# A gated linear attention and GELU FFN kernel: halved first load, full-width inter products, a fixed instruction list

## Chip, cores and metric

The kernel runs on one core of a Trainium2 chip. The metric is device time in microseconds, from launch to end. Its parts are TensorE (PE in the profile; PEld are its weight loads), VectorE (DVE), ScalarE (ACT), GpSimd (POOL), and SyncE (SP), which issues most of the DMA transfers. PSUM has eight banks of 128 x 512 float32 that TensorE writes into.

## The reference

Four batches, eight heads, 768 tokens, head size 48. A state of 48 x 48 per head decays per key channel and is read by the query; the result, 3072 tokens of 384, goes through an FFN of width 2048.

```python
f = 1.0 / (1.0 + np.exp(-f_logit))
for t in range(S):
    state = f[:, :, t, :, None] * state + np.einsum('bhd,bhe->bhde', k[:, :, t], v[:, :, t])
    y[:, :, t] = np.einsum('bhd,bhde->bhe', q[:, :, t], state)
x = y.transpose(0, 2, 1, 3).reshape(B * S, H * D)
h = x @ w_in
out = (0.5 * h * (1.0 + erf(h / sqrt(2)))) @ w_out
```

## The kernel before

The 3072 tokens are 24 chunks of 128; two chunks are a unit (0 to 11), and two chunks are also a group of the FFN (0 to 11). Six chunks, three units, make a batch, so chunks 0, 6, 12 and 18 start without a state. Matmuls take bf16.

In a chunk the recurrence becomes matmuls. Cumulated log decays g come from a triangular matmul. k times exp(-g) and q times exp(g) are formed, scores are k against q under a triangular mask, and y is masked scores times v plus q times the old state (the **inter** product). The state adds the chunk's k-v product and is scaled by the chunk's whole decay.

Every piece of work is recorded in a plan with engine, estimated duration, priority and the buffers it needs. `Plan.run` picks, in before, the piece that can start first by its estimates, priority deciding between near ones (with random offsets from `SEEDS`). The result is emitted as one fixed order for each engine. Each engine runs its own in order, so a piece that waits holds back all behind it on that engine. The names of the pieces, with chunk or unit number, are used below:

- E, L (lines 494, 497, ACT): exp and log of the logits of a unit, giving log decays. C (526, 527, 515 or 521, 523, PE): their cumulated sums. G (535, DVE): the second chunk's sums by subtraction, units 2 to 4.
- RG, GT, GL (543, 549, 570 or 565, ACT): exponentials for k, q and the state. KP, QP (576, DVE or POOL): the decayed k and q, in buffers sc. VC (583, POOL or ACT): v cast to bf16, buffers vb.
- Tk, Tq (611, PE): transposes into PSUM. KQ (617, DVE or ACT): the copy to buffer kq. From unit 4 on both are a DMA transpose instead, KD (599, issued by SP).
- A (784 or 722, PE): scores. AM (631, DVE): mask. S (806 or 745, PE): the k-v product of the state. R (651, 655, DVE), T (657, POOL), SB (662, POOL, two head halves): state sum, decay and bf16 copy.
- YI (826), YX (705): the masked product and the inter product of units 0 to 4; Y (758 and 699) both, for the others. YB (675, DVE or ACT): y to bf16. XT, X (691, 694) or a DMA transpose XD (679): y transposed for the FFN.
- F1.g.u (875): an eighth of the first FFN layer of group g, six matmuls of 256 columns into one of four PSUM banks. GE (885, ACT): GELU of that bank. F2.n.r (896): a quarter of the second layer of chunk n, four matmuls of 384 columns. O (901): the copy out of PSUM. Stores (906) go out on SP.

Units 0 to 4 (`PAIRS`) are pair units: each SBUF row holds two consecutive tokens, even and odd, so that loads move runs of 384 bytes; the two 64-row halves of a tile are then the two chunks. Units 5 to 11 are loaded chunk by chunk. In a pair unit kq holds, for each of the even and odd tokens, 128 columns of which 64 belong to each chunk. The inter product of a chunk therefore takes two matmuls of 64 columns for each of four head pairs:

```python
for j in range(2):
    nc.tensor.matmul(yp.t()[64 * j:64 * j + 64, 96 * p:96 * p + 96],
                     kq.t()[:, 1, p, j, 64 * cc:64 * cc + 64], osb.t()[:, p, :], ...)
```

Loads are issued in the order of `LOADS`: for unit 0 the logits (f0), then k0, v0, q0, then f1, v1, k1, q1, then on GpSimd the first weight piece i0 (1024 of the 2048 columns), and so on. `load` gates a change of issuing engine on an earlier transfer, so that i0 waits for f1, i1 for k2, and the logits f3 for weight piece o3.

ScalarE needs one function table for exp and log and another for GELU, so its order is made of stages of one kind with a table load (line 953) between. Filler matmuls on a zero tile (line 947, called junk) are put before pieces that the plan expects to start late in the first 30 us.

Of the kernel before, what the change touches and what calls it, by code (L numbers as in the profile page):

```python
# [15 lines left out]

# [8 lines left out]

SPREAD, SEED = (1.0, 97)

SEEDS = [1643, 41, 3215, 1275, 2533, 2502, 823, 887, 1264, 763, 2447, 3095]

NUDGE = {}  # L30
XA = 0.0
# [48 lines left out]
class Op:  # L80
    __slots__ = ("eng", "dur", "fn", "bufs", "prio", "deps", "table", "start", "end", "vis", "seq", "name",
                 "left", "outs", "inst", "chain", "opens", "lag", "lat", "port", "mode", "held")


class Plan:

# [3 lines left out]
    def add(self, eng, dur, fn, rd=(), wr=(), bufs=(), prio=0.0, deps=(), table=None, name="", chain=None, opens=None, lag=0.0, lat=None, port=False, mode=0, held=False):  # L92
# [5 lines left out]
        o.held = held  # L98
        o.seq = len(self.ops)
# [16 lines left out]
    def run(self):  # L116
        free = dict.fromkeys(list(LAT), 0.7)
        free["DMA"] = 1.8
        rng = random.Random(SEED)
        own = [random.Random(x) for x in SEEDS]  # L120
        for o in self.ops:
            if o.prio > -5:
                k = min(max(int(o.prio % 1000) // 20, 0), len(SEEDS) - 1)
                o.prio += rng.uniform(-SPREAD, SPREAD)
                if SEEDS[k]:
                    w = (0.5, 1.0, 3.0, 8.0)[SEEDS[k] % 4]
                    o.prio += own[k].uniform(-w, w)
            o.prio += NUDGE.get(o.name, 0.0) + (XA if o.table == "exp" and o.prio > 40 else 0.0)
# [9 lines left out]
        placed = []  # L138
        while ready:
            best = None  # L140
            for o in ready:
# [26 lines left out]
            if o.eng == "PE" and o.mode != mode:  # L168
                mode = o.mode
                d += TURN  # L170
# [29 lines left out]

SIZES = [2, 2, 2, 2, 2, 2, 2, 2, 2, 2, 2, 2]
PAIRS = [0, 1, 2, 3, 4]
WIN = [1024, 512, 512]
# [4 lines left out]
SPLIT = []  # L220
# [4 lines left out]
GKP, GQP = ([2], [3])  # L225
# [5 lines left out]
NGT = 4  # L231
GLD = []
# [3 lines left out]
AMX = []  # L236
WARM = 30.0
LOADS = ['f0', 'k0', 'v0', 'q0', 'f1', 'v1', 'k1', 'q1', 'i0', 'k2', 'f2', 'v2', 'q2', 'i1', 'i2', 'i3', 'o0', 'o1', 'o3', 'o2', 'f3', 'k3', 'q3', 'u4', 'v3']
LOADS += [f"u{n}" for n in range(12) if f"u{n}" not in LOADS and f"c{2 * n}" not in LOADS and f"f{n}" not in LOADS]


@with_exitstack
def kernel(
# [14 lines left out]
    NCH = B * nC  # L258
    d_model = moe_w_in.shape[0]
# [42 lines left out]
    s_rr, s_tn = slots(3, [C, P2, 2 * D], F32, "rr"), slots(3, [C, P2, 2 * D], F32, "tn")  # L302
    s_sb = slots(3, [C, P2, 2 * D], BF16, "sb")
    s_yb = slots(3, [C, 2, HD], BF16, "yb")
    s_os = slots(4, [C, d_model], F32, "osb")
    s_xT = {s: slots({1: 4, 2: 4}.get(s, 2), [C, s, KO, C], BF16, f"xT{s}") for s in set(SIZES)}
    s_gT = {s: slots({1: 4, 2: NGT}.get(s, 2), [C, FO, s * C], BF16, f"gT{s}") for s in set(SIZES)}
# [15 lines left out]

# [30 lines left out]
    for i in range(3):  # L354
        P.add("DVE", 0.2, lambda i=i: nc.vector.memset(
            s_sb.tiles[i].rearrange("p a b -> p (a b)").bitcast(F32), 0.0), wr=[f"sbz{i}"], prio=-70)
# [5 lines left out]
    z_sb = [f"sbz{i}" for i in range(3)]  # L362
# [7 lines left out]
    U = [dict(fl=s_fl.new(), lf=s_lf.new(), pair=u in PAIRS, **{nm: s_in[nm].new() for nm in s_in}) for u in range(NU)]  # L370
# [8 lines left out]

    order, pools = [], []  # L380

    def load(eng, issue, wr, bufs, dur, name):
        i = len(order)
        gate = None
        if i and order[i - 1][0] != eng:
            back = 4 if eng == "pool" else 2
            for j in range(i - back, -1, -1):
                if order[j][0] != eng:
                    gate = order[j][1]
                    break  # L390
# [10 lines left out]
        if prev is not None and order[-1][0] != eng:  # L401
            prev.lat = 2.2
        gd = [gate] if gate is not None else []
        if eng == "pool":
# [4 lines left out]
            k = P.add("POOL", 0.8, None, deps=gd, prio=-1000 + i, name="i" + name, lat=1.3)  # L409
# [10 lines left out]
    def src(a, n):  # L420
        b, c = divmod(n, nC)
        return a[b, :, c * C:(c + 1) * C, :].rearrange("h t d -> t h d")

    def srcp(a, u):
        b, c = divmod(2 * u, nC)
        return a[b, :, c * C:(c + 2) * C, :].rearrange("h (p j) d -> p h (j d)", j=2)

    win_src = moe_w_in.rearrange("(kk p) f -> p kk f", p=C)
    wo_src = moe_w_out.rearrange("(r p j) m -> r p j m", r=4, j=4)
    for what in LOADS:  # L430
        m = int(what[1:])
        if what[0] in "ucfkqv":
# [5 lines left out]
            if x["pair"]:  # L438
                assert what[0] != "c"
                for nm, a in names:  # L440
                    if what[0] not in ("u", nm[0]):
                        continue
                    if nm == "fl" and m in SPLIT:
                        for i in range(2):
                            load("sp", lambda x=x, a=a, m=m, i=i: nc.sync.dma_start(
                                out=x["fl"].t().rearrange("p (h x) -> p h x", h=H)[:, 4 * i:4 * i + 4], in_=srcp(a, m)[:, 4 * i:4 * i + 4]),
                                [("fl", 2 * m + i)], [x[nm]], 0.85, f"fl{m}.{i}")
# [12 lines left out]
        elif what[0] == "i" and m < len(WIN):  # L460
            load("pool", lambda m=m: nc.gpsimd.dma_start(out=win[m], in_=win_src[:, :, wcol[m]:wcol[m] + WIN[m]]),
                 [f"win{m}"], [], {512: 1.97, 1024: 3.95}[WIN[m]] + (0.5 if order[-1][0] == "sp" else 0.0), what)
# [4 lines left out]
    def decays(u):  # L467
# [33 lines left out]
        last = 2 * u + 1 if (2 * u + 1) % nC == nC - 1 else None  # L501
# [84 lines left out]

    St = {}

# [3 lines left out]
    def turn(u, kq):  # L592


        for j in range(2):
# [13 lines left out]
            def trans(i, tpv=tpv, sc=sc):  # L609
# [7 lines left out]
            P.add("ACT" if help_ else "DVE", 0.86 if help_ else 0.61, lambda tpv=tpv, j=j, help_=help_: copier(help_)(  # L617
                kq.t()[:, :, :, j, :].rearrange("a i p t -> a (i p) t"), tpv().rearrange("a i p t -> a (i p) t")),
# [17 lines left out]
    def carry(n, sp, mm, mmdur, mmrd, mmbufs, first_c):  # L636
# [16 lines left out]
        else:  # L653
            old = St["t"]
            P.add("DVE", 0.475, lambda: nc.vector.tensor_tensor(rr.t(), spf(), old.t(), ALU.add),  # L655
                  rd=[("sp", n), ("tn", n - 1)], wr=[("rr", n)], bufs=[sp, rr, old], prio=pr + PRI["S"] - 0.5, name=f"R{n}")
            P.add("POOL", 0.83, lambda: nc.gpsimd.tensor_tensor(tn.t(), rr.t(), glb(), ALU.mult),  # L657
                  rd=[("rr", n), ("gl", n)], wr=[("tn", n)], bufs=[rr, tn, gl], prio=pr + 2, name=f"T{n}")
        St["t"] = tn
# [42 lines left out]
    def interp(yp, kq, cc, osb):  # L702
        for p in range(P2):
            for j in range(2):
                nc.tensor.matmul(yp.t()[64 * j:64 * j + 64, 96 * p:96 * p + 96], kq.t()[:, 1, p, j, 64 * cc:64 * cc + 64],
                                 osb.t()[:, p, :], start=False, stop=False, skip_group_check=True)

    def attn_nat(u):
# [3 lines left out]
        for j in range(2):  # L712
# [11 lines left out]
            if u in AJ:  # L724
                both.append((n, amm, aps, ams))
                if j:
                    P.add("PE", 0.46, lambda both=tuple(both): [b[1]() for b in both], mode=1, rd=[("kq", n - 1), ("kq", n)],
# [5 lines left out]
            P.add("PE", 0.23, amm, mode=1, rd=[("kq", n)], wr=[("ap", n)], bufs=[kq] + aps + ams, prio=pr + PRI["A"], opens=aps[0], name=f"A{n}")  # L733
            mask_scores(aps, ams, ("am", n), f"AM{n}", ("ap", n), pr, mask, "mask")
        for j in range(2):
            n = 2 * u + j
            c, x, pr = n % nC, X[n], 10 * n
            sc, vb, ams = x["sc"], x["vb"], amss[j]
            osb = St.get("sb") if c else None
            if c < nC - 1:  # L740
# [6 lines left out]
                St["sb"] = carry(n, sp, smm, 0.175, [("kp", n), ("vb", n)], [sc, vb], c == 0)  # L747
# [4 lines left out]
            def ymm(j=j, ams=ams, vb=vb, yp=yp, osb=osb):  # L752
                if osb is not None:
                    inter(yp, lambda p: kq.t()[:, 1, p, j, :], osb, True)
                for hh in range(2):
# [6 lines left out]
                  rd=[("am", n, 0), ("am", n, 1), ("vb", n), ("kq", n)] + ([("sb", n - 1, 0), ("sb", n - 1, 1)] if c else []),  # L762
# [3 lines left out]
    def attn_pair(u):  # L766
# [6 lines left out]
        sps = [s_m.new(), s_m.new()] if (n0 + 1) % nC < nC - 1 else [s_m.new()]  # L773
        ams, both = [], []
        for jk in range(2):
# [3 lines left out]
            def amm(jk=jk, aps=aps):  # L779
                for p in range(P2):  # L780
                    for cc in range(2):
                        for hh in range(2):
                            r, t = slice(64 * hh, 64 * hh + 64), slice(64 * cc, 64 * cc + 64)
                            nc.tensor.matmul(aps[hh].t()[t, p * C:(p + 1) * C].rearrange("a (j t) -> a j t", j=2),  # L784
# [16 lines left out]
        def smm():  # L801
            for p in range(P2):
# [6 lines left out]
        P.add("PE", 0.45, smm, mode=1, rd=[("kp", n) for n in ns] + [("vb", n) for n in ns],  # L809
              wr=[("sp", n) for n in ns[:len(sps)]], bufs=sps + scs + vbs, prio=pr + PRI["S"], opens=sps[0], name=f"S{u}")  # L810
        osb = St.get("sb") if n0 % nC else None
        for cc in range(len(sps)):
            St["sb"] = carry(ns[cc], sps[cc], None, 0, None, None, ns[cc] % nC == 0)
            if not cc:
                mid = St["sb"]
# [16 lines left out]
        if u in YJ:  # L832
            olds = [(cc, o) for cc, o in enumerate((osb, mid)) if o is not None]

            def joint():
                intra()
                for cc, o in olds:
                    interp(yps[cc], kq, cc, o)
            P.add("PE", 0.5 + 0.2 * len(olds), joint, mode=1,
                  rd=rdi + [("kq", m) for m in ns] + [("sb", ns[cc] - 1, i) for cc, _ in olds for i in range(2)],  # L840
# [146 lines left out]
```

## Time and profile before

| what | us |
|---|---|
| median of 3 runs | 182.21 (181.89 to 182.56) |
| span of the profiled execution, first to last instruction | 181.1 |
| first FFN matmul starts | 20.67 |
| long dense run of F1 starts | 27.52 |
| TensorE's last matmul ends, then copy and store | 178.07 |
| L885 GELU on ScalarE | 57.5 for 96 |
| L875 first layer on TensorE | 68.7 for 576 |
| L896 second layer on TensorE | 66.0 for 368 |
| L953 table loads | 19.2 for 15 |
| L947 filler matmuls | 10.4 for 36 |

A group's busy time is the union of its instructions' times; matmuls are pipelined and overlap, so their mean duration is longer than their share of the engine. What a group costs TensorE is the next group's start less its own.

### The profile page before, as it was taken

The page shows a single profiled execution, that of the slowest core. Times are in us where ns is not written, and L with a number is a line of the kernel's source. Part 1 is how long each engine was busy: PE and PEld are TensorE (multiplying, and loading weights), DVE is VectorE, ACT ScalarE, POOL GpSimd, SP SyncE. Part 2 cuts the span into 40 slices and gives each one's busy share as a digit, 9 for nine tenths or more (in the row PEclk, how much of TensorE's full clock was granted, in tenths as well). Part 3 has the DMA queues.
Part 4 walks back from the last instruction along what each step waited for, and adds up shares of the span by engine and source line. Part 5 has one row for each costly group of instructions (what it writes and reads, how often), then busy time and mean ns, then how long its engine had stood idle before and what let it go on. Part 6 is the DMA issues. An engine that isn't in the chain of part 4 may idle for free.

```text
span 181.1 us, 4916 instructions
## 1 busy us (share of the span) xinstructions
PE 171.7 (95%) x1990; PEld 132.3 (73%) x1990; DVE 96.3 (53%) x194; ACT 125.2 (69%) x212; POOL 53.6 (30%) x116
## 2 busy tenths in 40 slices
PE   7788889999999999988999999999999999999993
PEld 2356669966787688785779689976697986886972
DVE  5289750058898564244896692527691625362110
ACT  2775198963899189999967759777585578560720
POOL 7657870003043641140176113112435110300000
PEclk9999999999999999999999999999999999999999
DMA  6999999949997898999999999999999872814102
GB/s 148 261 261 226 268 170 203 200 115 267 278 266 142 186 197 170 249 227 171 216 179 213 215 175 207 195 187 189 185 245 181 181 162 47 166 37 91 43 0 87
DMA packets 106998, 32.61 MB, mean 180 GB/s; under 512 B 102113, under 2 KB 106081, under 8 KB 106977
## 3 DMA queue, kind: packets, MB, share of 16 engines
q1 hardware_dynamic: 105056, 29.07, 79.7%
q0 software_dynamic: 1776, 3.15, 9.8%
q8 instruction: 15, 0.25, 0.6%
q10 hardware_dynamic: 144, 0.10, 0.2%
q14 instruction: 7, 0.05, 0.1%
HBM read 25.17 MB, written 4.72 MB: 165 GB/s over the span
## 4 chain that ended last, share of the span: by engine, by line
PE 64%; ACT 15%; DMA 15%; SPq 3%; issue 1%; DVE 0%; DVEq 0%
PE ps L875 26%; PE ps L896 25%; ACT gT L885 7%; DMA fl<-in_f_logit_dram 7%; DMA win<-in_moe_w_in_dram 5%; ACT L953 4%; SPq L449 3%; DMA kq<-sc 2%; PE ps L722 2%; PE ps L758 2%; PE ps L917 1%; ACT gt L549 1%; PE ps L521 1%; PE ps L699 1%; PE ps L745 1%
## 5 line engine op out<-in xcount | busy, mean ns | idle before, releaser
L885 ACT ACTIVATE gT<-ps 128x512 bf16<-128x512 f32 x96 | 57.5, 671 | 24.6 <-PE ps L875 23.0
L875 PE MATMUL ps<-xT,win 128*128 128x256 bf16 x576 | 68.7, 273 | 1.3 <-ACT gT L885 0.9
L896 PE MATMUL ps<-wout,gT 128*128 128x384 bf16 x368 | 66.0, 326 | 0.0
L875 PEld LDWEIGHTS <-win 128*128 128x128 bf16 x576 | 61.6, 114 | 3.9 <-issue 1.2
L896 PEld LDWEIGHTS <-gT 128*128 128x128 bf16 x368 | 34.2, 98 | 19.5
L583 POOL CAST vb<-vt 128x384 bf16<-128x384 f32 x22 | 12.6, 584 | 52.5 <-DMA vt<-in_v_dram 52.4
L631 DVE TENSOR_TENSOR am<-ps,mask 128x512 bf16<-128x512 f32 x28 | 17.6, 684 | 15.1 <-PE ps L722 15.1
L901 DVE COPY osb<-ps 128x384 f32<-128x384 f32 x20 | 11.1, 556 | 25.9 <-PE ps L896 18.2
L657 POOL TENSOR_TENSOR tn<-rr,gl 128x384 f32<-128x384 f32 x16 | 14.0, 872 | 35.2 <-DVE rr L655 34.6
L576 DVE TENSOR_TENSOR sc<-qt,gt 128x384 bf16<-128x384 f32 x23 | 14.0, 616 | 13.7 <-ACT gt L549 13.7
L576 DVE TENSOR_TENSOR sc<-kt,rg 128x384 bf16<-128x384 f32 x23 | 13.5, 597 | 11.3 <-ACT rg L543 11.3
L953 ACT ACT_TABLE_LOAD x15 | 19.2, 1283 | 0.3
L662 POOL CAST sb<-tn 48x192 bf16<-48x192 f32 x40 | 14.8, 371 | 11.6 <-DVE tn L651 6.6
L494 ACT ACTIVATE fl<-fl 128x768 f32<-128x768 f32 x12 | 10.1, 842 | 10.5 <-DMA fl<-in_f_logit_dram 10.5
L675 DVE CAST yb<-ps 128x384 bf16<-128x384 f32 x22 | 11.9, 555 | 7.4 <-PE ps L758 3.7
L631 DVE TENSOR_TENSOR am<-ps,maskp 128x512 bf16<-128x512 f32 x20 | 12.5, 684 | 2.2 <-PE ps L784 1.4
L543 ACT ACTIVATE rg<-ps 128x384 f32<-128x384 f32 x21 | 10.3, 503 | 4.4 <-PE ps L523 2.8
L549 ACT ACTIVATE gt<-ps 128x384 f32<-128x384 f32 x21 | 10.2, 503 | 3.9 <-PE ps L523 3.3
L947 PE MATMUL ps<-junk 128*128 128x512 bf16 (+3 forms) x36 | 10.4, 423 | 2.1 <-POOL junk L939 1.3
L655 DVE TENSOR_TENSOR rr<-ps,tn 128x384 f32<-128x384 f32 x16 | 8.9, 553 | 3.5 <-POOL tn L657 1.8
L497 ACT ACTIVATE lf<-fl 128x768 bf16<-128x768 f32 x12 | 10.1, 843 | 0.4
L947 PEld LDWEIGHTS <-junk 128*128 128x128 bf16 x36 | 3.6, 111 | 6.2 <-issue 3.5
(74 smaller groups left out, 130.4 us busy)
## 6 DMA issues: line engine op xcount, KB each, us to landing
out_dram<-osb SPq DMA_DIRECT2D x19, 192.0 KB, 3.1
fl<-in_f_logit_dram SPq DMA_DIRECT2D x14, 192.0 KB, 3.8
kt<-in_k_dram SPq DMA_DIRECT2D x14, 192.0 KB, 3.8
qt<-in_q_dram SPq DMA_DIRECT2D x14, 192.0 KB, 3.7
vt<-in_v_dram SPq DMA_DIRECT2D x14, 192.0 KB, 3.9
fl<-in_f_logit_dram SPq DMA_DIRECT2D x5, 384.0 KB, 6.2
kt<-in_k_dram SPq DMA_DIRECT2D x5, 384.0 KB, 6.2
vt<-in_v_dram SPq DMA_DIRECT2D x5, 384.0 KB, 5.7
```

The costliest lines, as they stand in the source:

```text
L549: P.add("ACT", 0.40, lambda g=gps[j], gtv=gtv: nc.scalar.activation(gtv(), g.t()[:, 0:HD].rearrange("q (p h d) -> q p h d", h=2, d=D), AF. ...
L576: P.add("POOL" if pl else "DVE", 0.80 if pl else 0.475, lambda a=a, y=y, j=j, w=w, pl=pl, b=(gtv if w else rg): (nc.gpsimd if pl else nc.v ...
L583: P.add("ACT" if hv else "POOL", 0.40 if hv else 0.47, lambda y=y, j=j, hv=hv: (nc.scalar.copy if hv else nc.gpsimd.tensor_copy)(y["vb"].t ...
L631: P.add("POOL" if pl else "DVE", 1.15 if pl else 0.61, lambda hh=hh, pl=pl: (nc.gpsimd if pl else nc.vector).tensor_tensor(ams[hh].t(), ap ...
L657: P.add("POOL", 0.83, lambda: nc.gpsimd.tensor_tensor(tn.t(), rr.t(), glb(), ALU.mult), rd=[("rr", n), ("gl", n)], wr=[("tn", n)], bufs=[r ...
L662: P.add("POOL", 0.36, lambda hh=hh: nc.gpsimd.tensor_copy(sb.t()[64 * hh:64 * hh + D, :, D * hh:D * hh + D], tn.t()[64 * hh:64 * hh + D, : ...
L675: P.add("ACT" if help_ else "DVE", 0.40 if help_ else 0.475, lambda: copier(help_)(yb.t()[:, i, :], yp.t()[:, 0:HD]), rd=[("yp", n)], wr=[ ...
L875: nc.tensor.matmul(hps.t()[:, i * tok:(i + 1) * tok].rearrange("a (s t) -> a s t", s=s), col(fo)[:, kk, :], xT.t()[:, :, kk, :], start=(kk ...
L885: nc.scalar.activation(to, fr, AF.Gelu)
L896: nc.tensor.matmul(op.t()[:, 0:d_model], gT.t()[:, fo, s_ * C:(s_ + 1) * C], wout[fo // 4][:, fo % 4, :], start=(fo == 0), stop=(fo == FO ...
L947: nc.tensor.matmul(o.opens.t()[:, 0:w], junk[:, 0:C], junk[:, 0:w], start=True, stop=True, skip_group_check=True)
L953: nc.scalar.preload_act_table_set({"exp": "natural_log_exp_and_others", "gelu": "gelu_and_others"}[o.table])
```

## The change

- `Plan.run` no longer chooses: it takes the pieces in the order of a list of 918 numbers, `ORDER`, and only the buffer a piece gets and the filler count still come from the estimates. `SEEDS`, `SPREAD`, `NUDGE` are gone. `PRIO` is empty.
- `SPLIT = [0]`: f0 is loaded as two transfers of four heads each, and E0 and L0 are two instructions each of four heads.
- In pair units outside `KDMA`, which are 0 to 3, the KQ copy sorts columns by chunk, so that the 128 columns of one chunk stand together. The inter product takes one full 128-column matmul for each head pair (24 fewer matmuls in all); the scores take the same number in the same sizes with other slices. Unit 4 keeps the half-width form.
- `NTN`, `NSB` = 7: seven buffers instead of three for the float32 state and for its bf16 copy, and four more memsets at the start.
- The durations in the plan (`after`, `mode`, weight loads) and the rule of `load`'s gates are changed; the gates fall on the same transfers as before.
- New functions for units loaded by head halves (`decays_hs`, `attn_hs`, `carry_hs`) are not called: the lists that select them, `HALVES` and `DENSE`, are empty.

```diff
+            for o in ([todo[len(placed)]] if todo else ready):
...
+SPLIT = [0]
+NTN, NSB = 7, 7
+HALVES = []
+DENSE = []
...
-    s_rr, s_tn = slots(3, [C, P2, 2 * D], F32, "rr"), slots(3, [C, P2, 2 * D], F32, "tn")
-    s_sb = slots(3, [C, P2, 2 * D], BF16, "sb")
+    s_rr, s_tn = slots(3, [C, P2, 2 * D], F32, "rr"), slots(NTN, [C, P2, 2 * D], F32, "tn")
+    s_sb = slots(NSB, [C, P2, 2 * D], BF16, "sb")
...
+            def evac(tpv=tpv, j=j, help_=help_):
+                if U[u]["pair"]:
+                    copier(help_)(kq.t().rearrange("a i p c (j r) -> a (i p) c j r", j=2)[:, :, :, j, :],
+                                  tpv().rearrange("a i p (c r) -> a (i p) c r", c=2))
+                    return
...
-    def interp(yp, kq, cc, osb):
+    def interp(yp, kq, cc, osb, full):
         for p in range(P2):
+            if full:
+                nc.tensor.matmul(yp.t()[:, 96 * p:96 * p + 96], kq.t()[:, 1, p, cc, :], osb.t()[:, p, :], start=False, stop=False, skip_group_check=True)
+                continue
...
+                            if u not in KDMA:
+                                nc.tensor.matmul(aps[hh].t()[t, p * C:(p + 1) * C], kq.t()[r, 0, p, cc, 64 * jk:64 * jk + 64],
+                                                 kq.t()[r, 1, p, cc, :], start=True, stop=True)
+                                continue
```

What the list does to the order, by the names above:

| where | before | after |
|---|---|---|
| PE, unit 1 and first FFN pieces | A1.1 A1.0 (filler) F1.0.1 F1.0.3 F1.0.2 YI1 YX2 YX3 F1.0.0 XT2 XT3 C4 (filler, 2304 columns) F1.1.3 | A1.1 (filler) F1.0.0 A1.0 F1.0.2 F1.0.3 YI1 YX2 YX3 F1.0.1 XT2 XT3 C4 (filler, 640 columns) F1.1.2 |
| ACT, units 3 and 4 | RG6 GT6 GL7 E4 L4 YB5 RG7 KQ6 X4 GT7 RG8 GT8 O3 RG9 GT9 GL9, GELU | RG6 GT6 GL7 RG7 GT7 E4 YB5 L4 X4 KQ6 GL9 GT8 RG8 RG9 GT9 O3, GELU |
| PE, group 2 | F1.2.5 Tq7 F1.2.0 F1.2.7 F1.2.3 A3 F1.2.1 | F1.2.0 A3 F1.2.7 F1.2.4 F1.2.3 S3 F1.2.6 |
| ACT, unit 5 | RG10 GT10 GL10 RG11 GT11, GELU | GT11 RG11 RG10 GL10 GT10 E6, GELU |
| PE, groups 3 and 4 | F2.4 and F2.5 before F1.3's last five; XT8 XT9 C10 C11 ... F1.4.0 F1.4.2 F2.6 S10 F1.4.4 F1.4.6 ... F2.7.0 F2.7.1 A11 | F1.3.4 F2.6.0 XT8 XT9 F2.4.0 F2.4.1 C10 F2.4.2 F2.4.3 F1.4.0 F1.4.3 F2.6.1 to F2.6.3 F1.4.4 F1.4.2 F1.4.6 F1.4.1 S10 F1.4.5 F1.4.7 F2.8.0 A11 |
| DVE, unit 5 | KP10 QP10 KP11 O6 R10 QP11 | QP11 KP11 QP10 KP10 O4 O6 R10 |
| POOL | T16 SB16 SB16 VC18 VC19; VC10 ... VC11 VC12 before VC14 | T16 SB16 SB15 SB15 VC18 VC19 SB16; VC10 ... VC14 SB9 VC11 VC12 |
| SP | stores among the loads of units 4 and 5 | loads of units 4 and 5 first; store of chunk 17 ahead of the last one |

## Prediction

> **What bounds the kernel now.** I read the busy shares first, then the chain that ended last in order of time, then TensorE's timeline where that chain leaves or re-enters TensorE, then ScalarE's.
>
> ```profile
> PE 171.7 (95%) x1990; PEld 132.3 (73%) x1990; DVE 96.3 (53%) x194; ACT 125.2 (69%) x212; POOL 53.6 (30%) x116
> PE   7788889999999999988999999999999999999993
> PEclk9999999999999999999999999999999999999999
> ```
>
> TensorE is the full engine, at an undiminished granted clock. A busy share of 95% says little alone, since a waiting stream can count as busy; so I compare how long equal groups take. Six first-layer matmuls (line 875) take 0.66 us back to back and four second-layer ones (line 896) 0.65. The chain shows where the dense part begins:
>
> ```profile
> 10.84 9.78 DMA win<-in_moe_w_in_dram
> ...
> 20.67 2.16 PE ps L875 x18
> ...
> 25.61 0.73 ACT gT L885
> 26.38 1.13 PE ps L947 x5
> 27.52 1.32 PE ps L875 x12
> ```
>
> The first FFN matmul stands at 20.67 because the first weight piece lands at 20.62. Four pieces fill the four FFN banks. Then TensorE waits for the first GELU, and **at 26.38, when a bank is free, it spends 1.13 us on filler matmuls** (line 947) ahead of the useful ones. Why GELU comes that late is in ScalarE's timeline:
>
> ```profile
> 22.56 0.84 ACT L494 ACTIVATE fl<-fl 128x768 f32<-128x768 f32 x1 [3.89 <-DMA fl<-in_f_logit_dram]
> 23.43 0.85 ACT L497 ACTIVATE lf<-fl 128x768 bf16<-128x768 f32 x1
> 24.30 1.28 ACT L953 ACT_TABLE_LOAD   x1
> 25.59 2.53 ACT L885 ACTIVATE gT<-ps 128x512 bf16<-128x512 f32 x4
> ```
>
> ScalarE sits 3.89 us until unit 2's logits land, does its two decay functions, loads the other table and only then starts GELU. From 27.52 to 178.07 TensorE is nearly gapless. Its exceptions, found by comparing equal groups, are these:
>
> ```profile
> 53.97 0.64 PE L784 MATMUL ps<-kq 64*64 64x128 bf16 x32
> 55.05 1.47 PE L875 MATMUL ps<-xT,win 128*128 128x256 bf16 x12 [0.44 <-ACT gT L885]
> ...
> 77.10 1.65 PE L875 MATMUL ps<-xT,win 128*128 128x256 bf16 x12
> 79.20 2.78 PE L875 MATMUL ps<-xT,win 128*128 128x256 bf16 x24 [0.45 <-ACT gT L885]
> 81.81 1.46 PE L896 MATMUL ps<-wout,gT 128*128 128x384 bf16 x8
> 83.38 0.40 PE L722 MATMUL ps<-kq 64*128 64x128 bf16 x8
> 84.14 0.40 PE L722 MATMUL ps<-kq 64*128 64x128 bf16 x8 [0.37 <-DMA kq<-sc]
> ```
>
> The first column is the start, so a group's real cost is the next start minus its own. The scores at 53.97 take 1.08 us against 0.57 for the same 32 at 62.74: 0.51 lost, waiting for GELU behind a table load. The 12 first-layer matmuls at 77.10 take 2.10 against 1.31: 0.79 lost, the same cause. The 8 at 81.81 take 1.57 against 1.30 and the scores behind them 1.09 against 0.56: 0.8 lost, waiting for unit 5's DMA transposes. Together 2.1 us; I found 0.2 more at 40.30 and no other gap over 0.15. So the change can gain (a) before 27.5, (b) in these waits, (c) by taking matmuls away. Behind 84.5 us little but (c) is left.
>
> **Logits by halves.** Unit 0's logits come as two transfers and two exp/log pairs. ScalarE starts exp at 4.56, when the whole tile has landed; five tiles land by 10.55 (the fifth is the logits of unit 1), so one tile takes (10.55 − 4.56)/4 = 1.5 us and half a tile 0.75. The first half should land at 3.8, its exp (0.84/2, about 0.45) lies before the second half's landing, and log ends near 5.9 where it ended at 6.27: 0.4 us earlier. [...] Either way the end barely moves: query decays wait for q, the fourth tile (about 9.05; DVE starts them at 9.22), and the first FFN matmul waits for the weights at 20.62, whose issue on GpSimd waits for unit 1's logits at 10.55 in both orders. The cover at that point is the 0.7 us of filler ahead of 20.67. I book 0, between −0.1 and +0.1. The extra issue on SP (0.4 to 0.5 us) is hidden: its later issues last 1.2 to 1.4 us each, paced by the transfers.
>
> **Full-width inter products** in units 0 to 3: 8 half-width matmuls become 4.
>
> ```profile
> 59.41 0.36 PE L705 MATMUL ps<-sb,kq 128*64 128x96 bf16 x8
> 59.70 1.47 PE L896 MATMUL ps<-wout,gT 128*128 128x384 bf16 x8
> ...
> 86.43 0.33 PE L699 MATMUL ps<-sb,kq 128*128 128x96 bf16 x4
> 86.60 0.36 PE L758 MATMUL ps<-vb,am 128*128 128x48 bf16 x8
> ```
>
> By starts, eight halves cost 0.29 us, sixteen 0.46; four full ones cost 0.17. So 0.12 is saved for each unit: twice behind 27.5 (units 2 and 3), 0.24 us, and twice in the start, hidden. A rule again speaks against it: "TensorEngine Tiling (Array Packing)", section "Key Properties", has different tiles run their loads and matmuls in parallel, which would make a pair of halves as cheap as one full matmul and the gain 0. Sixteen halves at 29 ns against 42 ns a full one show only a part of that. I take 0.24, ends 0 and 0.35. The permuted key/query layout that it needs changes the five DVE copies (0.68) and three ScalarE copies (1.0) in form alone: 1024 elements, inner runs of 64 instead of 128. No row shows that form; the bounds are no cost and 0.4 us a DVE copy. I take 0, since runs of 48 elements in the decay products show no such penalty (0.55 us for 384).
>
> **Seven state buffers.** GpSimd waited once, 3.0 us, for TensorE to release one, and TensorE did not wait for it. The four more DVE memsets (0.22 each) fit DVE's 4.6 us of idle before 7.75. Booked 0.
>
> **The fixed list** is the large part. In place of five fillers (2,304 columns) only two (640) stand at 26.38: 640/2304 of 1.13 is 0.3, so the 72 matmuls start at about 26.7, **0.85 earlier**, ends 0.5 and 0.9. The pieces needing later weights then come at 28.7; that piece lands about 28.6 (its first reader stood at about 29.5), so this just fits.
>
> The ScalarE stage from 36.31 to 52.96 has the same operations, but RG7 and GT7 (0.43 each) move ahead of E4, into the 2 us of idle before 46.70. Behind E4 6.26 us shrink to about 5.4, so GELU restarts near 53.4 instead of 54.26, while TensorE reaches the fifth piece later, S3 standing before it. **The 0.51 goes.** What is late next: YB5 now precedes L4 but still follows E4, so it ends near 48.0, and TensorE, 0.85 ahead, meets the transposes of chunk 5 at 47.7: **+0.45 new**.
>
> At the next stage E6 joins the exp functions: two tables 2.56, four at 0.4, gl 0.1, E6 0.85, 5.1 us against 4.3 before. But the list puts F2.4.0 to F2.4.3 (2.6) and C10 there. From F1.3.4's end TensorE has F2.6 (2.6), X transposes 0.33, F2.4 2.6, C10 0.27 and four first-layer pieces 2.6, 8.4 us, ahead of the first piece that needs a freed bank. **The 0.79 goes.** Scores A11 come after 3.4 us more of work, 11.8; the chunk-11 and chunk-10 decays now stand together on DVE without O6 and R10 (1.1 us) between, so the transposes end about 10.0 us after that same point. **The 0.8 goes.** The 0.2 at 40.30 goes too.
>
> Behind this I checked each first-layer stage in the new order against exp time plus 1.28 us of table; cover exceeds need by 0.3 (C22) to 2 us. Stores move later past loads on SP; the store of chunk 17 now stands ahead of the last one, but the third-last store issues at 176.10 for 0.33 us and the last at 178.53, so it fits. I allow **+0.45** for waits that I cannot see. The tail (178.07 to 181.1) is unchanged.
>
> **Sum:** −0.85 −0.51 −0.79 −0.8 −0.2 −0.24 + 0.45 + 0.45 = −2.5, and 0.1 to 0.2 more for one or two entries fewer into half-array work (eight second-layer matmuls ahead of such scores take 1.39 us instead of 1.30): −2.7. The profiled execution spans 181.1, so 178.4; the median, 182.21, lies 1.1 above the span, so **179.5**.
>
> **Rivals.** *Given back:* the start gains its 0.85 and 0.24, but ScalarE, in order, moves the waits elsewhere. For it: 4.7 us of ScalarE's 36–53 stage is waiting for logits that no reordering makes land earlier. Against: it was busy from 46.7 on. 182.2 − 0.85 − 0.24 is 181.1, and 180.6 with one 0.5 us wait gone as well: 180.6 to 181.3. *No change:* the logits at 22.54 hold GELU at 25.6 in both, and a few waits of 0.5 return; 181.3 to 183.1, about 182.2. *Slower:* on GpSimd, state copies now stand behind value casts: SB16's second half behind VC18 and VC19, VC11 behind VC14. The casts wait for their loads (52.4 us in 15 waits, the longest 8.4). Y17 comes 5.5 us behind A17, and the load's way takes about 7 of the 9 us since the transposes' issue, so 2 us is cover. With one wait of 8.4 TensorE loses 6.4: 179.5 + 6.4 = 185.9; it decides from a wait of 4.7. Against: the list issues fewer stores ahead of these loads. *Not what it says:* the half-head functions are never called, as their lists are empty; only the first unit's load is split.
>
> **Chances.** Full gain 0.62 (178.2 to 180.6), given back 0.14, no change 0.12, slower 0.12. About 0.5% (0.9 us) is what a measurement here can tell from none: faster 0.76, same 0.12, slower 0.12. The range 178.2 to 182.3 leaves out the slower case and a little below.
>
> **What would show it.** Right: long first-layer run from 26.7; no filler run of 1 us at 26.4; scores A3 and A11 at 0.57 and 0.56 us; 12 first-layer matmuls before the GELU restart at 1.31; lines 975 at 0.17 for four; TensorE's end near 175.4. Wrong: first-layer run still at 27.5, or TensorE waiting for GpSimd's sb or vb behind 80 us.

## The result, and the profile after

The changed kernel takes 181.37 us (median of 22 runs, 180.76 to 182.36), the kernel before beside it 182.11 (22 runs, 181.62 to 183.01): a ratio of 0.9958, interval 0.9943 to 0.9973. It is faster by 0.74 us, where 2.7 were forecast. The profiled execution spans 179.4 us against 181.1, which is 1.7 and not 0.74; where the other 0.9 is will turn out to be the largest error of the prediction. Three single executions in the experiments below (of split_alone, best and half_ns) took 279 to 345 us and are left out of every median.

The chain of waits of the changed kernel from 20 to 40 us, in order of time (start, duration, what):

```profile
12.40 10.34 DMA fl<-in_f_logit_dram
...
24.50 1.28 ACT L1247
...
25.79 0.76 ACT gT L1175
26.55 0.04 issue
26.59 0.43 PE ps L1241 x2
27.02 7.86 PE ps L1165 x72
```

The weights have left the chain; unit 2's logits head it. The filler (now line 1241) is down from 1.13 to 0.43 us and the long first-layer run (now line 1165) starts at 27.02 where the same view had 27.52: 0.50 gained, not 0.85. TensorE's timeline of the changed kernel at the places where before had its waits:

```profile
47.41 0.61 PE L876 MATMUL ps<-ident,sc 128*128 128x128 bf16 x8
48.13 0.60 PE L961 MATMUL ps<-ident,yb 128*128 128x128 bf16 x6
48.59 0.62 PE L876 MATMUL ps<-ident,sc 128*128 128x128 bf16 x8
...
51.62 0.84 PE L1058 MATMUL ps<-kq 64*64 64x128 bf16 x32
52.39 2.15 PE L1165 MATMUL ps<-xT,win 128*128 128x256 bf16 x18
54.48 0.51 PE L1093 MATMUL ps<-vb,sc 64*128 64x96 bf16 x16
55.29 1.47 PE L1165 MATMUL ps<-xT,win 128*128 128x256 bf16 x12 [0.30 <-ACT gT L1175]
...
76.33 2.78 PE L1165 MATMUL ps<-xT,win 128*128 128x256 bf16 x24
78.95 0.33 PE L1018 MATMUL ps<-vb,sc 128*128 128x96 bf16 x4
...
81.17 0.62 PE L995 MATMUL ps<-kq 64*128 64x128 bf16 x16
81.73 2.12 PE L1186 MATMUL ps<-wout,gT 128*128 128x384 bf16 x12
```

By starts: the scores behind 80 us take 0.56, and nothing waits at 76.33. But the scores at 51.62 take 0.77 and not 0.57, and 55.29 still waits 0.30 for GELU, so of that loss (0.51) nothing is saved. A new loss of 0.4 stands at 47.4 to 48.6: eight transposes take 0.72 where the next eight take 0.46, and six transposes of y 0.46 for 0.33. Behind 56 us, to TensorE's end at 175.97, no wait over 0.15 us is left.

### The profile page after: what moved, and what is told of

Same layout as the page of the kernel before. It is cut to its first block, busy times and chain, and to the rows that moved or that the text cites. A ratio compares the mean times of both kernels' runs of the same rounds, so it can differ in the third digit from the quotient of the medians.

```text
span 179.4 us, 4851 instructions
## 1 busy us (share of the span) xinstructions
PE 171.8 (96%) x1963; PEld 132.2 (74%) x1963; DVE 99.5 (55%) x198; ACT 125.2 (70%) x214; POOL 51.0 (28%) x116
## 4 chain that ended last, share of the span: by engine, by line
PE 76%; SPq 6%; ACT 6%; DMA 6%; DVE 2%; issue 2%; DVEq 0%; ACTq 0%
PE ps L1165 33%; PE ps L1186 31%; DMA fl<-in_f_logit_dram 6%; SPq L513 6%; PE ps L995 2%; PE ps L1031 2%; PE ps L1211 1%; PE ps L585 1%; PE ps L969 1%; DVE am L901 1%; PE ps L1018 1%; ACT gt L613 1%; ACT fl L558 1%; ACT rg L607 1%; ACT gT L1175 1%
## 5 line engine op out<-in xcount | busy, mean ns | idle before, releaser
L640 DVE TENSOR_TENSOR sc<-qt,gt 128x384 bf16<-128x384 f32 x23 | 15.4, 675 | 13.7 <-ACT gt L613 13.0
L647 POOL CAST vb<-vt 128x384 bf16<-128x384 f32 x22 | 11.8, 544 | 31.3 <-DMA vt<-in_v_dram 31.1
L932 POOL CAST sb<-tn 48x192 bf16<-48x192 f32 x40 | 14.3, 363 | 12.3 <-DVE tn L921 10.8
L640 DVE TENSOR_TENSOR sc<-kt,rg 128x384 bf16<-128x384 f32 x23 | 14.0, 622 | 4.3 <-ACT rg L607 4.3
L558 ACT ACTIVATE fl<-fl 128x768 f32<-128x768 f32 (+1 forms) x13 | 10.3, 796 | 5.6 <-DMA fl<-in_f_logit_dram 5.4
L561 ACT ACTIVATE lf<-fl 128x768 bf16<-128x768 f32 (+1 forms) x13 | 10.2, 795 | 0.3
```

The source lines that it names most:

```text
L558: nc.scalar.activation(v, v, AF.Exp, scale=-1.0)
L640: P.add("POOL" if pl else "DVE", 0.80 if pl else 0.475, lambda a=a, y=y, j=j, w=w, pl=pl, b=(gtv if w else rg): (nc.gpsimd if pl else nc.v ...
L932: P.add("POOL", 0.36, lambda hh=hh: nc.gpsimd.tensor_copy(sb.t()[64 * hh:64 * hh + D, :, D * hh:D * hh + D], tn.t()[64 * hh:64 * hh + D, : ...
```

## The experiments

All were timed beside the kernel before, 6 to 12 runs each but where said, and the ratio is to that before. The runs were taken on four chips (after_again to f2_first, old_order to few_fill, split_alone to before_again, c8_early to half_ns), on which before took 182.61, 182.15, 182.42 and 182.18. So medians from different chips compare only roughly.

| run | median, us | ratio, 95% interval | span of the profile |
|---|---|---|---|
| after_again | 181.31 | 0.9939 (0.9915 to 0.9963) | 179.2 |
| half_inter | 182.57 | 1.0008 (0.9986 to 1.0029) | 180.6 |
| no_split | 180.62 | 0.9897 (0.9870 to 0.9924) | 178.8 |
| f2_first | 180.98 | 0.9924 (0.9897 to 0.9951) | 179.4 |
| old_order | 181.92 | 0.9974 (0.9961 to 0.9988) | 180.0 |
| whole_16 | 180.97 | 0.9930 (0.9905 to 0.9955) | 178.9 |
| more_fill | 181.65 | 0.9976 (0.9959 to 0.9992) | 179.8 |
| few_fill | 181.82 | 0.9987 (0.9962 to 1.0012) | 179.8 |
| split_alone | 182.45 | 1.0001 (0.9981 to 1.0020) | 180.4 |
| warm_16 | 180.82 | 0.9893 (0.9862 to 0.9924) | 179.1 |
| best | 180.61 | 0.9891 (0.9860 to 0.9922) | |
| before_again | 182.36, one run | | 180.3 |
| c8_early | 180.61 | 0.9912 (0.9889 to 0.9934) | 178.8 |
| e4_c8 | 180.29 | 0.9890 (0.9865 to 0.9915) | 178.6 |
| half_ns | 181.44 | 0.9954 (0.9936 to 0.9971) | 179.7 |

**after_again** is the changed kernel once more, called the copy below.

> The changed kernel once more, for a second profiled execution beside the 22 measured times. Its first profile spans 179.4, 1.7 under the profile of before (181.1), while the medians differ by only 0.74 (181.37 against 182.11). If the first profile was a lucky execution, this one spans 180.0 to 180.6. If the profile shows less than the whole time, so that 1 us is lost outside the span, it spans 179.2 to 179.7 again and the time is again 181.3.

The second profile has the same losses at the same places, with the run's start at 26.38 on TensorE's timeline (26.86 in the first, 27.35 in before), since unit 2's logits landed 0.5 us earlier. The start of that run differs by half a microsecond between executions of one program.

**half_inter**: the half-width inter products and their column order, with the new list.

```diff
-                if U[u]["pair"]:
+                if False:
...
-                            if u not in KDMA:
+                            if False:
...
-                    interp(yps[cc], kq, cc, o, u not in KDMA)
+                    interp(yps[cc], kq, cc, o, False)
```

(the same in the second call of `interp`)

> Same list, but units 0 to 3 go back to the old key/query layout and two half-width inter matmuls for each head pair. My theory: 0.24 us slower than the changed kernel (0.12 each for units 2 and 3, behind the start of the long first-layer run), nothing from units 0 and 1. Rival, tiles that run beside each other: 0.0. Rival, the sorted copy costs VectorE and ScalarE time in the first 20 us: 0.2 to 0.5 faster than the changed kernel.

It came out 1.26 above the copy of the changed kernel, five times what the matmuls cost; taken up under old_order and half_ns. The sorted copies to kq take the same with and without the sorting, 0.68 us on VectorE and 1.01 on ScalarE.

**no_split**: the first logits in one load.

```diff
-SPLIT = [0]
+SPLIT = []
```

(and the three pieces of the second half taken out of the list)

> Same list without the second transfer and the second exp and log of unit 0: its logits come in one transfer. My theory: the same within 0.2 us, since the first FFN matmul waits for weights that land near 20.6 and GELU for the logits of unit 2. Rival, the split delays every later transfer (unit 2's logits landed at 22.74 in the changed kernel's profile, at 22.54 before): 0.2 faster, with the first GELU near 25.6.

It gained 0.69 on the copy: the split costs time, and this kernel beats before and the changed kernel. Some 0.2 of it is that 4 of the copy's 12 executions ran at a lower clock (0.991, see the end); its other eight have a median of 181.13. Where the rest is, is under whole_16 and split_alone.

**f2_first**: unit 2's logits loaded ahead of its keys.

```diff
-... 'i0', 'k2', 'f2', 'v2', ...
+... 'i0', 'f2', 'k2', 'v2', ...
```

> The changed kernel with unit 2's logits issued ahead of its keys, nothing else. My theory, that GELU's start is held by that transfer: the logits land 1.5 us earlier (near 21.3), GELU starts near 24.3 instead of 25.8, and the long first-layer run starts when TensorE gets there, near 26.6 to 26.8 instead of 27.0: 0.2 to 0.4 faster. Rival, the start is held elsewhere (transposes of chunks 2 and 3, decay sums of unit 2): no change, run at 27.0.

GELU starts at 24.34 in place of 25.79, but the long run only at 26.51, 0.13 later than in the copy: TensorE is busy with its own products until then, with no filler between. ScalarE's and TensorE's timelines:

```profile
24.34 2.55 ACT L1175 ACTIVATE gT<-ps 128x512 bf16<-128x512 f32 x4
...
26.22 0.34 PE L579 MATMUL ps<-negp,lf 128*128 128x1 bf16 x8
26.51 2.16 PE L1165 MATMUL ps<-xT,win 128*128 128x256 bf16 x18
```

The median fell by 0.33, inside the intervals.

**old_order**: the full-width products alone. The changed kernel's code, before's plan written into `ORDER`, no split, three state buffers.

```diff
-NTN, NSB = 7, 7
+NTN, NSB = 3, 3
-SPLIT = [0]
+SPLIT = []
-31 3 30 10 32 18 ...
+0 5 7 8 9 10 ...
```

> The full-width inter products alone: the changed kernel with the order of before's plan written into its list, the first logits in one load, three state buffers, and before's fillers to within 128 columns. The prediction booked 0.24 us for them (two units of 0.12 behind 27.5 us), so about 182.3 where before takes 182.6. The rival is what the half-width run against the changed kernel showed (182.57 against 181.31): the full width is worth about 1.2 us, then about 181.4 here. At 181.4 or below, the new order as a whole has brought next to nothing.

The difference of the medians is 0.23 us, the ratio's interval gives 0.2 to 0.7. Part of that may be chance: 10 of the 29 executions of before beside it span over 180.5 us and none of these 12 does, and against the other 19 (median 182.06) the difference is 0.14. In the traces, by starts, the inter products of units 2 and 3 take 0.46 and 0.29 us in before, 0.35 and 0.18 here: 0.22 less, near the forecast's 0.24. Those of unit 2, in before and here:

```profile
47.56 0.53 PE L705 MATMUL ps<-sb,kq 128*64 128x96 bf16 x16
48.02 0.62 PE L611 MATMUL ps<-ident,sc 128*128 128x128 bf16 x8
```

```profile
47.53 0.51 PE L975 MATMUL ps<-sb,kq 128*128 128x96 bf16 x8
47.88 0.61 PE L876 MATMUL ps<-ident,sc 128*128 128x128 bf16 x8
```

**whole_16**: chunk 16 stored by one transfer in place of two, the split kept.

```diff
-ROWS = [16, 17, 18, 19]
+ROWS = [17, 18, 19]
```

> The changed kernel with the rows of chunk 16 stored by one transfer in place of two: one transfer of the hardware queues fewer, so that the last store signs off on the semaphore that SyncE's closing checks take last, as in before, while the first logits stay split. Theory: the time from TensorE's last matmul to the end falls from 3.43 to about 3.0 us and the median by 0.4, to about 180.9. Rival: the split costs at the start, and the closing checks are nothing: 181.3 and 3.4 us at the end.

180.97, and from TensorE's last matmul (175.87) to the end (178.87) 3.00 us against 3.43. SyncE's waits near the end (line waited in, for what, total, times, longest), first of the changed kernel, then of this one:

```profile
SPq L1276 <- DMA out_dram<-osb: 1.2, 1, 1.2
```

```profile
SPq L1276 <- DMA out_dram<-osb: 0.8, 1, 0.8
```

The trace's event records say why. Each transfer that SyncE and ScalarE issue reports its completion on one of eight semaphores (counters that an engine can wait for). SyncE closes the program by checking these eight in a fixed order, about 0.06 us each. In the changed kernel the last store reports on the one checked first: SyncE waits there from 176.84 to 178.08 and then does seven more checks, to 178.55. In before the last store is on the one checked last, and the other checks pass while it is in flight. The semaphores are dealt out in turn: before has 128 such transfers, 16 for each, the changed kernel 129, so its last one is on the first again. One transfer more anywhere shifts all behind it by one.

**more_fill** and **few_fill**: before's filler in the changed kernel, the changed kernel's in before.

```diff
+                if o.name == "F1.1.2":
+                    room = 18
                 while room > 0:
```

```diff
+                if o.name == "F1.1.3":
+                    room = 5
                 while room > 0:
```

> The changed kernel with before's 2,304 filler columns in place of 640 ahead of the long first-layer run, nothing else. The prediction's step: the run then starts about 0.7 to 0.85 us later and all behind it too, so about 182.1. The theory now: ScalarE's stage from 36 to 54 us ends when it ends, since it waits for loads and for VectorE; the fifth batch of first-layer pieces restarts at about 55.0 in either case and the time stays at 181.3, within 0.2.

> The kernel before with 640 filler columns in place of 2,304 ahead of its long first-layer run, nothing else. The prediction's step: 0.7 to 0.85 us gained to the end, about 181.8 where before takes 182.6. The theory now: the run starts near 26.7, and the gain is gone at the wait for GELU at 55 us, so 182.6 within 0.2.

The new theory fell: the gain is not lost at the wait for GELU at 55 us, which stays as long as it was (0.30 in more_fill, 0.44 in few_fill). ScalarE's stage moves with the run's start. TensorE's timeline of more_fill, then of whole_16:

```profile
26.21 1.13 PE L1243 MATMUL ps<-junk 128*128 128x512 bf16 x4
27.18 1.58 PE L1165 MATMUL ps<-xT,win 128*128 128x256 bf16 x13
```

```profile
26.49 0.43 PE L1241 MATMUL ps<-junk 128*128 128x512 bf16 x2 [0.34 <-ACT gT L1175]
26.76 2.02 PE L1165 MATMUL ps<-xT,win 128*128 128x256 bf16 x17
```

In more_fill the run starts 0.42 later, and TensorE ends 0.52 later. From the first GELU to the run it is 1.83 us and 1.07 in whole_16, so the filler itself is worth 0.76, all of it carried to the end; GELU happened to start 0.34 earlier.

In before's order only about half arrives. In few_fill the run starts 0.96 us earlier than in the second profile of before (0.26 of it because GELU did); the lead is 0.98 at 55 us and 0.48 at TensorE's end. Of what is lost, 0.36 goes at unit 5's scores, which now come before their transposes have landed:

```profile
82.10 0.40 PE L722 MATMUL ps<-kq 64*128 64x128 bf16 x8
82.68 0.40 PE L722 MATMUL ps<-kq 64*128 64x128 bf16 x8 [0.18 <-DMA kq<-sc]
83.01 2.12 PE L896 MATMUL ps<-wout,gT 128*128 128x384 bf16 x12
```

By medians few_fill gains 0.33 us (interval: a loss of 0.2 to a gain of 0.7). More_fill is 0.68 above whole_16 on the same chip, of which some 0.4 is the tail.

**split_alone**: old_order plus the split.

> The full-width products in before's order, as in the run of the old order, plus the first logits in two loads and two exp/log pairs, nothing else. The prediction booked between -0.1 and +0.1 us for the split, so 181.9 where the old order took 181.92 and before takes 182.15. The theory now: 0.43 at SyncE's closing checks and 0.1 to 0.2 from later loads, so about 182.5, with 3.4 us from TensorE's last matmul to the end. If executions at a granted clock of 0.991 turn up here too, they belong to the split and not to the list.

Near what the theory has: 0.5 us above old_order by the ratios, TensorE's end at 176.99 against 177.00, and 3.43 us from there to the end against 3.02. At the start the keys, values and queries of unit 0 land about 0.6 us later (the queries at 9.40 against 8.80), but none of that reaches TensorE's end. So in this order the split costs 0.4 us, at the closing checks.

**before_again**: a second profile of before.

> The kernel before once more, for a second profile. Its spans lie in two clusters, about 180.0 to 180.5 and 180.7 to 181.2; the profile that the prediction read was 181.1, in the upper. Theory: in an execution of the lower cluster the scores behind 83 us take 0.56 us and not 1.09, and the eight second-layer matmuls ahead of them 1.40 and not 1.57; the waits at 54 and 77 us are there in both. Rival: the clusters differ in something else, at the start or the end, and that wait is there in both.

TensorE's timeline, then SyncE's issues:

```profile
79.09 2.78 PE L875 MATMUL ps<-xT,win 128*128 128x256 bf16 x24 [0.46 <-ACT gT L885]
81.70 1.46 PE L896 MATMUL ps<-wout,gT 128*128 128x384 bf16 x8
83.10 0.62 PE L722 MATMUL ps<-kq 64*128 64x128 bf16 x16
83.65 2.12 PE L896 MATMUL ps<-wout,gT 128*128 128x384 bf16 x12
```

```profile
74.68 0.70 SPq L457 DMA_DIRECT2D fl<-in_f_logit_dram  x1
76.89 3.10 SPq L599 DMA_TRANSPOSE kq<-sc  x2
```

The same two rows in the first profile of before:

```profile
76.97 0.90 SPq L457 DMA_DIRECT2D fl<-in_f_logit_dram  x1
77.98 3.14 SPq L599 DMA_TRANSPOSE kq<-sc  x2
```

The wait of 0.8 us at 81.8 to 84.5 is not there: the eight matmuls take 1.40 by starts and the scores 0.55. From the run's start to TensorE's end it is 149.87 us, against 150.71 in the profile that the prediction read; the difference is that wait. In the first profile SyncE was 2.3 us late with the loads ahead of the transposes, and issued them 1.1 late; why was not settled. The wait at 79.09 is there in both. Of 87 timed executions of before 52 span at most 180.5 us, and 35 more than that. That all of these 35 pay this wait is inferred from the two profiles. The profile of old_order, in which the scores take 0.55 too and none of whose executions spans over 180.1, agrees.

**warm_16**: whole_16 with more filler in the first 11 us.

```diff
+                room = {"C1": 45, "Tk0": 10, "A0.1": 15}.get(o.name, room)
                 while room > 0:
```

> The kernel with chunk 16 stored whole, with before's or more filler columns ahead of the first products (5,760 in place of 5,376, 1,280 in place of 896, 1,920 in place of 1,536). Theory: the executions at a granted clock of 0.991 (2 of 6 there, 5 of 12 in the changed kernel's copy, none of 53 of the kernel before) come from TensorE standing idle in the first 11 us, and go; then no run under 0.995 and a median of 180.7. Rival: the cause is elsewhere, and about one run in four or more is at 0.991 still.

No run of 6 is at 0.991 and the median is 180.82, as the theory has it (the copy had four such runs in 12; five is the count of the changed kernel's first 22). With a chance of some 1 in 5 per run that is weak evidence; see the end.

**best**: no_split, f2_first and no filler ahead of the long run.

```diff
-... 'i0', 'k2', 'f2', 'v2', ...
+... 'i0', 'f2', 'k2', 'v2', ...
...
+                if o.name == "F1.1.2":
+                    room = 0
                 while room > 0:
```

> What the runs so far would keep, in one kernel: the changed kernel with the first logits in one load, unit 2's logits loaded ahead of its keys, and no filler ahead of the long first-layer run. If the gains add: 180.62 (no split) less 0.33 (logits first) less about 0.27 (the two fillers) is about 180.0. If the bank that the first GELU frees sets the run's start and the logits' place gives nothing, 180.6.

180.61, as no_split: the gains do not add. With the logits first, f2_first's trace has no filler ahead of the run, and TensorE's own work sets its start. That this holds here too is not shown.

**c8_early** and **e4_c8** ask why the GELU wait at 54 us stayed. ScalarE in the changed kernel:

```profile
44.74 0.49 ACT L607 ACTIVATE rg<-ps 128x384 f32<-128x384 f32 x1 [2.42 <-DVE am L901]
45.13 0.48 ACT L613 ACTIVATE gt<-ps 128x384 f32<-128x384 f32 x1
46.23 0.18 ACT L634 ACTIVATE gl<-ps 128x8 f32<-128x8 f32 x1 [0.62 <-DVE g L599]
...
51.05 0.18 ACT L634 ACTIVATE gl<-ps 128x8 f32<-128x8 f32 x1 [0.69 <-DVE g L599]
...
53.20 1.28 ACT L1247 ACT_TABLE_LOAD   x1
54.50 1.34 ACT L1175 ACTIVATE gT<-ps 128x512 bf16<-128x512 f32 x2
```

The list put chunk 7's decays ahead of E4, and they need VectorE's subtraction (line 599), which itself comes after GT6: in the chain of waits GT6 ends at 45.62 and the subtraction runs from 45.64 to 46.21. On no_split, the pieces are moved in the list: for c8_early L4 and C8 ahead of the transposes of chunk 7, for e4_c8 E4 (and its load) ahead of GL7 as well.

```diff
-... 350 349 183 401 402 ...
+... 401 402 350 349 183 ...
```

```diff
-... 342 340 60 341 ... 400 ... 350 349 183 401 402 ...
+... 60 400 342 340 341 ... 401 402 350 349 183 ...
```

> The changed kernel with unsplit first logits, and in its list the log of unit 4 and the sums C8 moved ahead of the transposes of chunk 7 and four second-layer matmuls. In the profile without the split ScalarE sat 0.62 us at 45.90 and 0.70 us at 50.72 waiting for VectorE's subtractions, and its stage ended at 52.87. Theory: the second of these waits goes, the stage ends 0.4 to 0.5 us earlier, the wait of TensorE at 55 us (0.30) goes, and the median falls from 180.62 by 0.3. Rival: the stage's end is held by other things (PSUM banks, the copies of keys), and nothing changes.

> As the run with C8 early, and the exp of unit 4 put into ScalarE's first wait, ahead of the decays of chunk 7. Theory: both waits go if the logits have landed by 45.2, the stage ends 0.8 to 1.0 us earlier than 52.87, and both TensorE losses there (0.20 in the scores, 0.30 before the first-layer run at 55) go: 180.62 less 0.5 is about 180.1. Rival: the logits or VectorE hold it, and it is as with C8 alone or 180.6.

C8 alone gave nothing (180.61). On ScalarE the second wait of 0.7 became one of 0.63 before the next decay, at 51.49. On TensorE the loss at 55 us is gone, but C8, now earlier, waits for the log itself:

```profile
48.80 0.32 PE L590 MATMUL ps<-lf,trip 128*128 128x384 bf16 x1 [0.40 <-ACT lf L561]
```

With E4 ahead the first wait is gone. ScalarE in no_split, then in e4_c8:

```profile
54.16 1.35 ACT L1181 ACTIVATE gT<-ps 128x512 bf16<-128x512 f32 x2
```

```profile
45.30 0.84 ACT L558 ACTIVATE fl<-fl 128x768 f32<-128x768 f32 x1
46.04 0.18 ACT L634 ACTIVATE gl<-ps 128x8 f32<-128x8 f32 x1
...
51.18 0.52 ACT L607 ACTIVATE rg<-g 128x384 f32<-128x384 f32 x1 [0.62 <-DVE g L599]
...
53.79 1.95 ACT L1175 ACTIVATE gT<-ps 128x512 bf16<-128x512 f32 x3
```

GELU restarts 0.37 us earlier, TensorE ends 0.28 earlier (175.56 against 175.84), and the median is 180.29, the lowest of all. Each of its six runs is below each of c8_early's six on the same chip (179.98 to 180.38, 180.49 to 180.80). So the place of chunk 7's decays in the list held about 0.3 of the 0.5 us. ScalarE's longer wait, 2.2 to 2.8 us ahead of RG6 at 44.74, is there in all these runs, and nothing was tried against it.

**half_ns**: half_inter without the split.

> The new list without the split, with the half-width inter products and their column order of before. In the old order the full width was worth 0.23 us; in the new list with the split, 1.26. Theory: the products are worth 0.24 by themselves, and the rest was chance waits and executions at 0.991 of the clock, so about 180.9 where the list without the split takes 180.62. Rival: the half width really costs over 1 us in the new order, because something there has no cover: 181.6 or more, with waits at 104 and 141 us in the profile.

0.8 above no_split and above c8_early, which was on the same chip (180.61): closer to the rival. TensorE at the second of two places:

```profile
140.50 0.40 PE L1001 MATMUL ps<-kq 64*128 64x128 bf16 x8
141.20 0.40 PE L1001 MATMUL ps<-kq 64*128 64x128 bf16 x8 [0.30 <-DMA kq<-sc]
141.53 0.74 PE L1171 MATMUL ps<-xT,win 128*128 128x256 bf16 x5
```

The scores of chunk 17 wait 0.48 for their DMA transposes in both half-width kernels, and in none of the nine other profiles of the new list whose span is given here, and a product near 104 us loses 0.2 to 0.3. In the new order the half width thus costs its 0.22 and about 0.7 in waits 40 to 80 us later. Why those transposes land later was not settled, nor what the further 0.4 us of half_inter are. The seven state buffers were not tried apart from the list.

## Why the prediction was right and wrong

The sign and most of the places were right, the size was not. That 181.37 lies in the range is owed to its width: it reached to 182.3, past no gain at all. Step by step, from TensorE's rows, with before_again for the usual execution of before:

| step | booked | measured |
|---|---|---|
| start of the long run | -0.85 | -0.52 (-1.00 in after_again, where the logits landed earlier) |
| scores A3 and GELU at 54 | -0.51 | 0 |
| 77.1 | -0.79 | -0.79 |
| transposes at 81.8 to 84.5 | -0.8 | 0 in before_again, -0.84 in the other |
| full-width products | -0.24 | -0.22 (old_order) |
| new wait at 47.7 | +0.45 | +0.4 |
| tail | 0 | +0.4 |
| 40.30 and fewer turns | -0.35 | -0.15, what is left of the sum |
| unseen waits | +0.45 | 0 behind 56 us |

In all the span falls from 180.28 to 179.40, by 0.88, near the 0.74 of the medians. The profile of the changed kernel is itself somewhat short: its 22 executions have a median span of 179.6.

**The step that failed first is "The 0.8 goes" together with "the median, 182.21, lies 1.1 above the span".** The wait was real in the profiled execution and the list does remove it, but before's second profile does not have it. The runs show that within one execution of before the time lies 1.96 us above the span (median of 87). A median only 1.1 above the profiled span thus meant that this execution was about 0.85 longer than a usual one: something in its trace was not in the median. Adding 1.1 to a changed span of 178.4 credited the change with that 0.85; with 1.96 the same span gives 180.4. The other 1.0 us to the measured 181.37 is in the next steps.

**The tail, put down as unchanged,** failed by 0.4, since one transfer more moves the last store to the semaphore checked first (whole_16, split_alone). The split was weighed for its landing and its issue; the later loads did land 0.5 us later (unit 0's queries at 9.58 against 9.05), which was called hidden and did not reach the end. Its count was not weighed.

**"The 0.51 goes"** failed because the decays moved into ScalarE's idle time were counted by their durations, not by what they wait for: the subtraction on VectorE. Taking E4 ahead of them gave 0.3 us (e4_c8); the other 0.2 is open. The prediction had GELU restart at 53.4; it came at 54.50.

**The start** was mis-sized by 0.33: GELU starts at 25.79 and not 25.59, and the shorter filler still occupies 0.43 in the chain, not 0.3. That the filler sets the start is right (more_fill); the later theory, that the gain is lost by 55 us, fell.

**The full width** was right in size, but the reading behind it was not. In before eight halves cost 0.29 us and sixteen 0.46, so the second eight cost 0.17, as much as four full ones. A further pair of halves thus costs no more than a full matmul, which agrees with the rule that the prediction had set against the change (the Trainium skill, "TensorEngine Tiling (Array Packing)", section "Key Properties"). What the full width saves is about 0.11 us for each group, whether of eight halves (0.29 to 0.18) or of sixteen (0.46 to 0.35). What these 0.11 are, no row shows.

**The allowance of 0.45 for unseen waits** was not needed behind 55 us. No rival came true as told. The time lies between *given back* (180.6 to 181.3) and the lower end of *no change* (181.3 to 183.1), but the start's gain was not lost in ScalarE's order, and TensorE nowhere waits for GpSimd behind 56 us.

## What to carry to other kernels

Before a wait of the profiled execution is booked as a gain, see whether that execution is a usual one: compare the median's distance from its span with the same distance in single runs, or take a second profile. Count transfers as well as bytes when a load is split, since the last store's place in the closing order can cost more than the load gains. A piece moved into an engine's idle time fills it only if what it reads is ready there; follow its inputs on the other engines first.

## What the hardware showed unexpectedly

The closing checks: 0.4 us at the end of a kernel from the number of transfers alone.

A granted clock of 0.990 to 0.991 as the mean of an execution occurs in the new list with the split: in 5 of the changed kernel's first 22 runs, in 4 of 12 of after_again (which take 181.83 to 182.32 against 180.73 to 181.57 for the rest), and in 11 of 55 of the six such kernels among the experiments. It occurs in none of 34 runs of that list without the split, of 35 in before's order, or of 87 of before. The split alone does not bring it about (split_alone, none of 11), and two kernels with both did not show it (f2_first, none of 7; warm_16, none of 6). No execution of that kind was profiled, and the cause is open.

The time outside the span is 1.96 us in before (median of 87; 1.87 to 1.98 in the kernels in its order) and 1.77 in the new list (1.72 to 1.85 in all its runs), a gain of 0.2 us that no view of the span shows. Its cause was not looked for.
